# Memory attention with a SwiGLU block: values of batch 1 loaded ahead of the weights, summed transposed and scaled in U, and gates begun on the gate weights alone

## Chip, core and metric

One core of a Trainium2 chip runs the whole program. The time is that of one execution on the device in microseconds, as a median of several runs. A stage is timed inside a profiled execution, on that execution's own clock, which starts at its first instruction.

## The reference, cut to what matters

```python
# q, k, v: (8 batches, 8 heads, 576 tokens, 64)    phi: (8, 8, 576, 32 memories)
a = exp(phi);  a = a / sum(a over tokens)           # the maximum is taken off first; it cancels
k_m = einsum('bhsm,bhsd->bhmd', a, k);  v_m = einsum('bhsm,bhsd->bhmd', a, v)
attn = softmax(q @ k_m.T / 8 over the 32 memories);  x = heads of (attn @ v_m) side by side
g = x @ w_gate;  val = x @ w_val;  out = (silu(g) * val) @ w_out
```

The kernel never forms x. It multiplies each head's v_m by that head's 64 rows of the weights once per batch, which gives U, a matrix of (head, memory) by feature, and then g = attn @ U. U has to be built for the gate weights and for the value weights, in three chunks of 512 features.

## The kernel before

Batches 0 and 1 form the start: they are computed slot by slot, alternating, while the weights and all inputs still come in. A slot is one block of 128 features by 288 tokens: two matmuls for the gate, a Silu on ScalarE, two matmuls for the values, a product on VectorE. The value part of a slot runs one slot late. The parts that matter (cut):

```python
def v_items(b):                     # values: sum by (head, memory), divide, transpose
    def sums():
        p = ps.tile([128, NG * D], FP32, tag="b", name="p_kv")
        kv_sum(b, p, (1,))                                   # 48 matmuls
        v_norm(b, p.rearrange("p (g d) -> p g d", g=NG))     # VectorE, times 1/sum
    return [sums, lambda: kv_T(b, (1,))]                     # TensorE transpose, VectorE copy

def u_round(b, parts, evac):        # U of some weights: 8 matmuls, two PSUM banks a part
    ...
    for (t, p), e in zip(banks, evac):
        if e == "a":
            nc.scalar.copy(out=t, in_=p)
        else:
            nc.vector.tensor_copy(out=t, in_=p)

def gv_slot(b, s):                  # gate and Silu, then the value part of the slot before
    ...

# the schedule from the first U on
run([u_both_halves(0, 0, 0)])                      # gate and value weights, features 0 to 255
warm(6)                                            # dummies
run(g0[:3] + v1[:1] + g0[3:4] + v1[1:])            # batch 1's values amid batch 0's slots
run([u_both_halves(1, 0, 0)] + g1[:3])
...
for c in range(1, NCH):                            # features 512 to 1023, 1024 to 1535
    s = 8 * c
    run([u_item(0, c)] + g1[s - 2:s] + g0[s:s + 4])
    run([u_item(1, c)] + g0[s + 4:s + 8] + g1[s:s + 6])
```

PSUM gives six banks to all of this. A full U round (512 features, gate and value) takes four of them and gives them back when ScalarE and VectorE, two banks each, have copied them out. `warm(n)` is n dummy matmuls that keep TensorE running.

The softmax here doesn't subtract the row's maximum and nothing guards it: scores larger than these inputs give would overflow.

Of the kernel before, what the change touches and what calls it, by code (L numbers as in the profile page):

```python
# [14 lines left out]
def kernel(  # L15
# [48 lines left out]
    phis, kvs, qs, qTs = {}, {}, {}, {}  # L64
    Q_SLOT = (0, 1, 0, 0, 1, 0, 1, 0)

    def load_phi(b, eng):
        t = inp.tile([P, H, J * M], FP32, tag="phi", name="t_phi")
        eng.dma_start(out=t, in_=phi[b].rearrange("h (p j) m -> p h (j m)", p=P))
        phis[b] = t  # L70
# [80 lines left out]
    box = {}  # L151
# [110 lines left out]
    def k_items(b):  # L262


        def sums():
            box["k"] = ps.tile([128, NG * D + NG], FP32, tag="b", name="p_kv")
            kv_sum(b, box["k"], (0,))

        def norm():
            kv_denominators(b, box["k"], NG * D)  # L270
            kv_reciprocal(b, box["k"], NG * D)
            k_norm(b, box["k"][:, 0:NG * D].rearrange("p (g a d) -> p g a d", g=NG, a=1))

        return [sums, norm, lambda: kv_T(b, (0,))]

    def v_items(b):


        def sums():
            p = ps.tile([128, NG * D], FP32, tag="b", name="p_kv")  # L280
            kv_sum(b, p, (1,))
            v_norm(b, p.rearrange("p (g d) -> p g d", g=NG))

        return [sums, lambda: kv_T(b, (1,))]
# [65 lines left out]

    def u_round(b, parts, evac):

        banks = []
        for which, c, halves in parts:
            f0, f1 = HC * halves[0], HC * (halves[-1] + 1)
            p = [ps.tile([128, CH], FP32, tag="b", name=f"p_u{g}") for g in range(NG)]
            for i in range(NP):
                for g in range(NG):
                    nc.tensor.matmul(  # L359
                        p[g][32 * i:32 * i + 32, f0:f1],  # L360
                        lhsT=kTs[b][64 * g:64 * g + 64, 2, 32 * i:32 * i + 32],
                        rhs=W[which, c][64 * g:64 * g + 64, halves[0]:halves[-1] + 1, i],
                        start=True,
                        stop=True,
                        tile_position=(64 * g, 32 * i),
                    )
            for g in range(NG):
                if (b, which, c, g) not in Us:
                    Us[b, which, c, g] = upool.tile(
                        [128, CH], BF16, tag=f"U{which}{c}{g}", name="t_U"  # L370
                    )
                banks.append((Us[b, which, c, g][:, f0:f1], p[g][:, f0:f1]))
        for (t, p), e in zip(banks, evac):
            if e == "a":
                nc.scalar.copy(out=t, in_=p)  # L375
            else:
                nc.vector.tensor_copy(out=t, in_=p)  # L377
# [5 lines left out]
    def flush_mul():  # L383
        while pend:
            pend.pop(0)()

    def gv_half(b, s, which):
# [4 lines left out]
        for g in range(NG):  # L392
            nc.tensor.matmul(  # L393
                p[:, 0:HALF],
                lhsT=Us[b, which, c, g][:, 128 * o:128 * (o + 1)],
# [6 lines left out]
    def gv_slot(b, s):  # L402
# [5 lines left out]
        sg = work.tile([128, HALF], BF16, tag="sg", name="t_sg")  # L408
        nc.scalar.activation(out=sg, in_=gate, func=AF.Silu)  # L409
        flush_mul()  # L410
# [8 lines left out]

    def u_buffers(b):  # L420

        n = 0
        for which in range(2):
            for c in range(NCH):
                for g in range(NG):
                    Us[b, which, c, g] = hpool.tile([128, CH], BF16, tag=f"h{n}", name="t_U")
                    n += 1
# [88 lines left out]
    def u_item(b, c, evac="avav"):  # L516

        both = ((0, c, (0, 1)), (1, c, (0, 1)))
        return lambda: u_round(b, both, evac)

    def u_both_halves(b, c, half, evac="avav"):

        both = ((0, c, (half,)), (1, c, (half,)))
        return lambda: u_round(b, both, evac)

    def u_half(b, which, c, half, evac):
        return lambda: u_round(b, ((which, c, (half,)),), evac)


    def u_three(b):  # L530

        u_round(b, ((0, 0, (0, 1)), (1, 0, (0, 1)), (0, 1, (0, 1))), "avavav")

    def u_values(b):

        u_round(b, ((1, 1, (0, 1)),), "vv")
# [27 lines left out]
    load_phi(1, nc.scalar)  # L564
    load_k(0)
# [11 lines left out]
    for which in range(2):  # L577
        load_w(which, 0, 0)
    load_v(1)
    for which in range(2):  # L580
        load_w(which, 0, 1)
    for c in range(1, NCH):
# [15 lines left out]
    exp_tables()  # L598
    warm(140)
    phi_exp(0)  # L600
    phi_exp(1)
    k0, k1, v0, v1 = k_items(0), k_items(1), v_items(0), v_items(1)
    q0, q1 = q_items(0, "vava"), q_items(1, "vvvv")
    run(k0[:2])
    warm(8)
    run(k0[2:])
    warm(14)
    run(q0[:2])
    warm(5)
    scores(0, 0)  # L610
    run(q0[2:])
    warm(5)
    scores(0, 1)
    warm(3)
    z_inv(0, 0)
    run(k1[:2])
    run(q1[:1])
    z_inv(0, 1)
    run(k1[2:] + q1[1:2])
# [5 lines left out]
    z_inv(1, 0)  # L625
    warm(2)
    scores(1, 1)
    warm(17)
    z_inv(1, 1)
    norm(1, 0)  # L630
    nc.scalar.preload_act_table_set("silu_and_others")  # L631
    run(v0[:1])
    warm(8)
    run(v0[1:])
    norm(1, 1)


    g0, g1 = gv_slots(0), gv_slots(1)
    warm(6)
    run([u_both_halves(0, 0, 0)])  # L640
    warm(6)
    run(g0[:3] + v1[:1] + g0[3:4] + v1[1:])
# [109 lines left out]
```

## Time and profile before

| | before |
|---|---|
| median of the three runs known before the prediction (a fourth, in the first set, makes it 249.71) | 249.81 us (249.41 to 250.35) |
| first gate, profiled run | 27.38 us |
| first matmul of the output projection, which ends the stage of batches 0 and 1 | 57.28 us |
| span | 248.2 us |

### The profile page before, as it was taken

The numbers are of one execution on the slowest core, as the hardware profiler recorded it, in microseconds if no ns is written. First come the engines' busy times: TensorE is split into PE (matmuls) and PEld (weight loads), VectorE is DVE, ScalarE is ACT, GpSimd is POOL, SyncE is SP. The second block draws the span as 40 slices with busy tenths as digits, with TensorE's granted clock in tenths as the row PEclk, the third lists the DMA queues.
The fourth block names the chain that finished last, engine by engine and source line by source line (L and its number), as shares of the span: only waits on it lengthen the run. The fifth ranks groups of instructions, "written<-read, shape, count | busy, mean of one in ns | idle before, by whom it ended". The sixth has DMA issues, their size and how long they took to land.

```text
span 248.2 us, 6645 instructions
## 1 busy us (share of the span) xinstructions
PE 237.2 (96%) x2595; PEld 152.2 (61%) x2622; DVE 158.3 (64%) x339; ACT 166.0 (67%) x360; POOL 54.5 (22%) x85
## 2 busy tenths in 40 slices
PE   7999899999999999999999999999999999999993
PEld 7976566775544766467645666476546655467543
DVE  0027699994437788488856778478846876587420
ACT  2449688886077667966896577966896577676201
POOL 8434355000060002260505240080007000000000
PEclk9999999999999999999999999999999999999999
DMA  7999999999699973999699689589525311310143
GB/s 184 205 203 201 198 198 201 233 210 184 136 158 247 239 172 62 177 251 219 88 221 250 96 122 237 154 155 157 92 55 130 56 42 45 85 42 3 42 128 86
DMA packets 49168, 37.00 MB, mean 149 GB/s; under 512 B 15984, under 2 KB 43888, under 8 KB 49136
## 3 DMA queue, kind: packets, MB, share of 16 engines
q0 software_dynamic: 27632, 22.42, 57.1%
q1 hardware_dynamic: 20496, 13.37, 23.5%
q10 hardware_dynamic: 1008, 0.79, 1.2%
q8 instruction: 20, 0.33, 0.6%
q14 instruction: 12, 0.10, 0.1%
HBM read 42.47 MB, written 9.44 MB: 209 GB/s over the span
## 4 chain that ended last, share of the span: by engine, by line
PE 92%; ACT 3%; issue 2%; DVE 1%; DMA 1%
PE p_oo L449 35%; PE p_g L393 20%; PE p_v L393 19%; PE p_u L359 5%; PE p_oo L560 5%; PE p_kv L177 2%; PE p_g L316 1%; PE p_g L336 1%; DMA out_dram<-t_o 1%; PE p_v L336 1%; PE p_kv L197 1%; ACT L631 1%; ACT t_qT L303 0%; PE p_q L292 0%; PE p_T L241 0%
## 5 line engine op out<-in xcount | busy, mean ns | idle before, releaser
L449 PE MATMUL p_oo<-WO,t_h 128*128 128x512 bf16 x393 | 101.6, 379 | 3.0 <-issue 2.9
L409 ACT ACTIVATE t_sg<-p_g 128x288 bf16<-128x288 f32 x192 | 77.6, 413 | 32.3 <-PE p_g L393 24.6
L416 DVE TENSOR_TENSOR t_h<-t_sg,p_v 128x288 bf16<-128x288 bf16 x192 | 84.9, 452 | 20.5 <-PE p_v L393 16.0
L393 PEld LDWEIGHTS <-t_U 128*128 128x128 bf16 x768 | 74.0, 98 | 30.8 <-issue 1.4
L393 PE MATMUL p_g<-t_A,t_U 128*128 128x288 bf16 x384 | 78.0, 286 | 1.1 <-ACT t_U L375 0.7
L393 PE MATMUL p_v<-t_A,t_U 128*128 128x288 bf16 x384 | 77.2, 286 | 0.0
L449 PEld LDWEIGHTS <-t_h 128*128 128x128 bf16 x420 | 39.6, 98 | 41.0 <-issue 6.0
L377 DVE CAST t_U<-p_u 128x512 bf16<-128x512 f32 (+1 forms) x58 | 34.8, 646 | 7.3 <-PE p_u L359 7.3
L461 DVE COPY t_o<-p_oo 128x512 f32<-128x512 f32 x27 | 18.6, 690 | 31.4 <-PE p_oo L449 31.3
L375 ACT CAST t_U<-p_u 128x512 bf16<-128x512 f32 (+1 forms) x46 | 22.7, 554 | 10.8 <-PE p_u L359 10.6
L93 POOL DMA_DIRECT2D t_q<-in_q_dram x6 | 4.7, 780 | 63.0 <-DMA t_qT<-t_q 62.2
L560 PE MATMUL p_oo<-bones 128*128 128x128 bf16 x218 | 16.6, 240 | 1.5 <-DVE bones L572 1.5
L459 ACT COPY t_o<-p_oo 128x512 f32<-128x512 f32 x8 | 4.7, 588 | 19.7 <-PE p_oo L449 19.5
L359 PE MATMUL p_u<-W,t_kT 64*32 64x512 bf16 (+1 forms) x416 | 15.8, 365 | 0.7 <-DVE t_kT L243 0.7
L560 PEld LDWEIGHTS <-bones 128*128 128x128 bf16 x218 | 14.9, 109 | 2.3 <-DVE bones L572 1.5
L146 ACT ACTIVATE t_ephi<-t_phi 96x768 bf16<-96x768 f32 x16 | 12.5, 844 | 4.2 <-DMA t_phi<-in_phi_dram 4.2
L160 POOL COPY t_mark<-t_A 1x1 bf16<-1x1 bf16 x4 | 0.7, 180 | 52.5 <-DVE t_A L345 52.5
L207 DVE RECIPROCAL t_rS<-p_kv 128x2 f32<-128x2 f32 x8 | 1.4, 171 | 16.5 <-PE p_kv L197 13.6
L345 DVE TENSOR_TENSOR t_A<-t_E,t_lz 128x576 bf16<-128x576 bf16 x16 | 11.5, 750 | 0.4 <-ACT t_lz L340 0.4
L340 ACT ACTIVATE t_lz<-t_lz 128x576 f32<-128x576 f32 x16 | 10.9, 683 | 0.5
L164 POOL TENSOR_TENSOR t_es<-t_es,t_ephi 96x256 f32<-96x256 f32 x16 | 10.7, 667 | 1.3
L359 PEld LDWEIGHTS <-t_kT 64*32 64x32 bf16 x416 | 4.8, 89 | 9.5 <-issue 7.0
(52 smaller groups left out, 156.1 us busy)
## 6 DMA issues: line engine op xcount, KB each, us to landing
t_kv<-in_k_dram POOLq DMA_DIRECT2D x8, 576.0 KB, 10.1
t_kv<-in_v_dram POOLq DMA_DIRECT2D x8, 576.0 KB, 14.5
out_dram<-t_o SPq DMA_DIRECT2D x23, 192.0 KB, 3.0
t_phi<-in_phi_dram POOLq DMA_DIRECT2D x6, 576.0 KB, 15.5
t_q<-in_q_dram POOLq DMA_DIRECT2D x6, 576.0 KB, 7.9
out_dram<-t_o SPq DMA_DIRECT2D x24, 128.0 KB, 2.4
W<-in_moe_w_gate_dram POOLq DMA_DIRECT2D x6, 256.0 KB, 13.1
W<-in_moe_w_val_dram POOLq DMA_DIRECT2D x6, 256.0 KB, 12.7
```

The source lines that it names most:

```text
L146: nc.scalar.activation(out=t[:, :, g].rearrange("p j i m -> p i j m"), in_=src[:, g], func=AF.Exp)
L340: nc.scalar.activation(out=lz, in_=lz, func=AF.Exp, scale=-1.0)
L345: nc.vector.tensor_tensor(out=a, in0=es.pop((b, g)), in1=lzs.pop((b, g)), op=ALU.mult)
L359: nc.tensor.matmul(p[g][32 * i:32 * i + 32, f0:f1], lhsT=kTs[b][64 * g:64 * g + 64, 2, 32 * i:32 * i + 32], rhs=W[which, c][64 * g:64 * g ...
L375: nc.scalar.copy(out=t, in_=p)
L377: nc.vector.tensor_copy(out=t, in_=p)
L393: nc.tensor.matmul(p[:, 0:HALF], lhsT=Us[b, which, c, g][:, 128 * o:128 * (o + 1)], rhs=atts[b, g][:, r], start=(g == 0), stop=(g == NG - 1),)
L409: nc.scalar.activation(out=sg, in_=gate, func=AF.Silu)
L416: nc.vector.tensor_tensor(out=dst, in0=sg, in1=val, op=ALU.mult)
L449: nc.tensor.matmul(mine["p"], lhsT=hts[c, jf][:, 128 * u:128 * (u + 1)], rhs=WO[jf], start=(jf == 0), stop=(jf == NJF - 1),)
L461: nc.vector.tensor_copy(out=t_o, in_=mine["p"])
L560: nc.tensor.matmul(p[:, 0:128], lhsT=bones, rhs=bones, start=True, stop=True)
```

## The change

The intent is to get rid of the stop that batch 1's values make amid the first gates. Its v is loaded before the weights, so its sum can run before the first gate. The sum is built transposed, so that neither a division nor a TensorE transpose follows it; the division by the sum of a moves into U's copies, whose partitions are (head, memory). The first gates need only the gate weights' U, so they begin before the value weights have landed. Dummies fill TensorE up to there. The core of the diff, with cuts:

```diff
-        def sums():
-            p = ps.tile([128, NG * D], FP32, tag="b", name="p_kv")
-            kv_sum(b, p, (1,))
-            v_norm(b, p.rearrange("p (g d) -> p g d", g=NG))
-        return [sums, lambda: kv_T(b, (1,))]
+    def v_direct(b):
+        p = ps.tile([128, NP, M], FP32, tag="b", name="p_vT")
+        for i in range(NP):
+            for j in range(J):
+                for g in range(NG):
+                    nc.tensor.matmul(p[64 * g:64 * g + 64, i],
+                        lhsT=kvs[b][:, 1, 2 * i + g, j * D:(j + 1) * D],
+                        rhs=ephis[b][:, j, g, i], ...)
+        nc.vector.tensor_copy(out=kTs[b][:, 2], in_=p.rearrange("p i m -> p (i m)"))
+        scaled.add(b)
...
             if e == "a":
-                nc.scalar.copy(out=t, in_=p)
+                if r is None:
+                    nc.scalar.copy(out=t, in_=p)
+                else:
+                    nc.scalar.activation(out=t, in_=p, func=AF.Copy, scale=r)
+            elif r is None:
+                nc.vector.tensor_copy(out=t, in_=p)
             else:
-                nc.vector.tensor_copy(out=t, in_=p)
+                nc.vector.tensor_scalar(out=t, in0=p, scalar1=r, scalar2=None, op0=ALU.mult)
...
     load_v(0)
-    for which in range(2):
-        load_w(which, 0, 0)
     load_v(1)
-    for which in range(2):
-        load_w(which, 0, 1)
-    for c in range(1, NCH):
+    for c in range(NCH):
         for half in range(2):
             for which in range(2):
                 load_w(which, c, half)
...
-    run([u_both_halves(0, 0, 0)])
-    warm(6)
-    run(g0[:3] + v1[:1] + g0[3:4] + v1[1:])
-    run([u_both_halves(1, 0, 0)] + g1[:3])
-    run([u_both_halves(0, 0, 1)] + g1[3:4] + g0[4:7])
-    run([u_both_halves(1, 0, 1)] + g0[7:8] + g1[4:6])
+    v_direct(0)
+    ...
+    warm(24)
+    v_direct(1)
+    warm(4)
+    run([u_half(0, (0,), 0, 0, "av"), u_half(1, (0,), 0, 0, "av")])
+    warm(6)
+    for s in range(4):
+        gv_gate(0, s)
+    run([u_half(0, (1,), 0, 0, "va"), u_half(1, (1,), 0, 0, "va")])
+    for s in range(2):
+        gv_gate(1, s)
+    flush_mul(3)
+    run([u_half(0, (0, 1), 0, 1, "va")])
+    flush_mul(2)
+    run(g1[2:4])
+    run([u_half(1, (0, 1), 0, 1, "av")] + g0[4:8] + g1[4:5])
     for c in range(1, NCH):
         s = 8 * c
-        run([u_item(0, c)] + g1[s - 2:s] + g0[s:s + 4])
-        run([u_item(1, c)] + g0[s + 4:s + 8] + g1[s:s + 6])
+        run([u_item(0, c)] + g1[s - 3:s] + g0[s:s + 5])
+        run([u_item(1, c)] + g0[s + 5:s + 8] + g1[s:s + 5])
```

U is also laid out with gate and value in one tile, for all batches. Further up, the denominators go ahead of k's sum, q's copies of batch 0 all go to VectorE, and 130 dummies open the program in place of 140.

More of the change, by code (lines that the diff above doesn't have):

```diff
@@ L64, with load_phi @@
     phis, kvs, qs, qTs = {}, {}, {}, {}
+    box = {}
     Q_SLOT = (0, 1, 0, 0, 1, 0, 1, 0)
-    def load_phi(b, eng):
+    def load_phi(b, *engs):
         t = inp.tile([P, H, J * M], FP32, tag="phi", name="t_phi")
-        eng.dma_start(out=t, in_=phi[b].rearrange("h (p j) m -> p h (j m)", p=P))
+        n = H // len(engs)
+        for i, eng in enumerate(engs):
+            eng.dma_start(
+                out=t[:, n * i:n * (i + 1)],
+                in_=phi[b, n * i:n * (i + 1)].rearrange("h (p j) m -> p h (j m)", p=P),
+            )
         phis[b] = t
@@ L149, in phi_exp @@
         ephis[b] = t
-    box = {}
     esums = {}
@@ L262, in k_items, with denominators @@
     def k_items(b):
-        def sums():
-            box["k"] = ps.tile([128, NG * D + NG], FP32, tag="b", name="p_kv")
-            kv_sum(b, box["k"], (0,))
-        def norm():
-            kv_denominators(b, box["k"], NG * D)
-            kv_reciprocal(b, box["k"], NG * D)
-            k_norm(b, box["k"][:, 0:NG * D].rearrange("p (g a d) -> p g a d", g=NG, a=1))
-        return [sums, norm, lambda: kv_T(b, (0,))]
-    def v_items(b):
+        def denominators():
+            p = ps.tile([128, NG], FP32, tag="b", name="p_S")
+            kv_denominators(b, p, 0)
+            kv_reciprocal(b, p, 0)
         def sums():
             p = ps.tile([128, NG * D], FP32, tag="b", name="p_kv")
-            kv_sum(b, p, (1,))
-            v_norm(b, p.rearrange("p (g d) -> p g d", g=NG))
-        return [sums, lambda: kv_T(b, (1,))]
+            kv_sum(b, p, (0,))
+            k_norm(b, p.rearrange("p (g a d) -> p g a d", g=NG, a=1))
+        return [denominators, sums, lambda: kv_T(b, (0,))]
+    def v_direct(b):
[3 more added lines that the diff above has]
+                for g in range(NG):
+                    nc.tensor.matmul(
+                        p[64 * g:64 * g + 64, i],
+                        lhsT=kvs[b][:, 1, 2 * i + g, j * D:(j + 1) * D],
+                        rhs=ephis[b][:, j, g, i],
+                        start=(j == 0),
+                        stop=(j == J - 1),
+                        tile_position=(0, 64 * g),
+                    )
+        nc.vector.tensor_copy(out=kTs[b][:, 2], in_=p.rearrange("p i m -> p (i m)"))
+        scaled.add(b)
     def q_T(b, g, n, eng="v"):
@@ L349 @@
     Us = {}
+    scaled = set()
     def u_round(b, parts, evac):
@@ L354, in u_round @@
         for which, c, halves in parts:
-            f0, f1 = HC * halves[0], HC * (halves[-1] + 1)
-            p = [ps.tile([128, CH], FP32, tag="b", name=f"p_u{g}") for g in range(NG)]
-            for i in range(NP):
-                for g in range(NG):
-                    nc.tensor.matmul(
-                        p[g][32 * i:32 * i + 32, f0:f1],
-                        lhsT=kTs[b][64 * g:64 * g + 64, 2, 32 * i:32 * i + 32],
-                        rhs=W[which, c][64 * g:64 * g + 64, halves[0]:halves[-1] + 1, i],
-                        start=True,
-                        stop=True,
-                        tile_position=(64 * g, 32 * i),
-                    )
@@ L367, in u_round @@
-            for g in range(NG):
-                if (b, which, c, g) not in Us:
-                    Us[b, which, c, g] = upool.tile(
-                        [128, CH], BF16, tag=f"U{which}{c}{g}", name="t_U"
-                    )
-                banks.append((Us[b, which, c, g][:, f0:f1], p[g][:, f0:f1]))
-        for (t, p), e in zip(banks, evac):
-            if e == "a":
-                nc.scalar.copy(out=t, in_=p)
+            w0, w1, h0, h1 = which[0], which[-1] + 1, halves[0], halves[-1] + 1
@@ new lines, in u_round @@
+            n = (h1 - h0) * HC
+            p = [
+                ps.tile([128, 2, HC], FP32, tag="b", name=f"p_u{g}").rearrange("p a f -> p (a f)")
+                for g in range(NG)
+            ]
+            for w in which:
+                o = (w - w0) * n
+                for i in range(NP):
+                    for g in range(NG):
+                        nc.tensor.matmul(
+                            p[g][32 * i:32 * i + 32, o:o + n],
+                            lhsT=kTs[b][64 * g:64 * g + 64, 2, 32 * i:32 * i + 32],
+                            rhs=W[w, c][64 * g:64 * g + 64, h0:h1, i],
+                            start=True,
+                            stop=True,
+                            tile_position=(64 * g, 32 * i),
+                        )
@@ new lines, in u_round @@
+            for g in range(NG):
+                if (b, c, g) not in Us:
+                    Us[b, c, g] = upool.tile([128, 2, 2, HC], BF16, tag=f"U{c}{g}", name="t_U")
+                if len(which) == 1:
+                    dst = Us[b, c, g][:, h0:h1, w0]
+                else:
+                    dst = Us[b, c, g][:, h0]
+                src = p[g][:, 0:(w1 - w0) * n].rearrange("p (a f) -> p a f", f=HC)
+                banks.append((dst, src, rSs[b][:, g, 0] if b in scaled else None))
+        for (t, p, r), e in zip(banks, evac):
+            if e == "a":
+                if r is None:
+                    nc.scalar.copy(out=t, in_=p)
+                else:
+                    nc.scalar.activation(out=t, in_=p, func=AF.Copy, scale=r)
+            elif r is None:
+                nc.vector.tensor_copy(out=t, in_=p)
@@ L376, in u_round, with flush_mul @@
             else:
-                nc.vector.tensor_copy(out=t, in_=p)
+                nc.vector.tensor_scalar(out=t, in0=p, scalar1=r, scalar2=None, op0=ALU.mult)
     hts = {}
     pend = []
-    def flush_mul():
-        while pend:
+    def flush_mul(n=None):
+        for _ in range(len(pend) if n is None else n):
             pend.pop(0)()
@@ L394, in gv_half @@
                 p[:, 0:HALF],
-                lhsT=Us[b, which, c, g][:, 128 * o:128 * (o + 1)],
+                lhsT=Us[b, c, g][:, o // 2, which, 128 * (o % 2):128 * (o % 2 + 1)],
                 rhs=atts[b, g][:, r],
@@ L400, in gv_half, with gv_gate @@
         return p[:, 0:HALF]
-    def gv_slot(b, s):
+    def gv_gate(b, s):
         jf, r = s // 2, s % 2
@@ L407, in gv_slot @@
         gate = gv_half(b, s, 0)
-        sg = work.tile([128, HALF], BF16, tag="sg", name="t_sg")
+        sg = work.tile([128, HALF], BF16, tag="sg", bufs=8, name="t_sg")
         nc.scalar.activation(out=sg, in_=gate, func=AF.Silu)
-        flush_mul()
         col = (b % 2) * S + r * HALF
@@ L418, in gv_slot @@
         pend.append(mul)
+    def gv_slot(b, s):
+        n = len(pend)
+        gv_gate(b, s)
+        flush_mul(n)
     def u_buffers(b):
-        n = 0
-        for which in range(2):
-            for c in range(NCH):
-                for g in range(NG):
-                    Us[b, which, c, g] = hpool.tile([128, CH], BF16, tag=f"h{n}", name="t_U")
-                    n += 1
+        for c in range(NCH):
+            for g in range(NG):
+                Us[b, c, g] = hpool.tile([128, 2, 2, HC], BF16, tag=f"h{2 * c + g}", name="t_U")
     def token_segments(t0, count):
@@ L516, in u_item @@
     def u_item(b, c, evac="avav"):
-        both = ((0, c, (0, 1)), (1, c, (0, 1)))
-        return lambda: u_round(b, both, evac)
-    def u_both_halves(b, c, half, evac="avav"):
-        both = ((0, c, (half,)), (1, c, (half,)))
-        return lambda: u_round(b, both, evac)
+        return lambda: u_round(b, (((0,), c, (0, 1)), ((1,), c, (0, 1))), evac)
     def u_half(b, which, c, half, evac):
@@ L530, in u_three @@
     def u_three(b):
-        u_round(b, ((0, 0, (0, 1)), (1, 0, (0, 1)), (0, 1, (0, 1))), "avavav")
+        u_round(b, (((0,), 0, (0, 1)), ((1,), 0, (0, 1)), ((0,), 1, (0, 1))), "avavav")
     def u_values(b):
-        u_round(b, ((1, 1, (0, 1)),), "vv")
+        u_round(b, (((1,), 1, (0, 1)),), "vv")
     def run(items):
@@ L564 @@
     load_phi(1, nc.scalar)
+    exp_tables()
+    phi_exp(0)
+    phi_exp(1)
     load_k(0)
@@ L576 @@
     load_v(0)
-    for which in range(2):
-        load_w(which, 0, 0)
     load_v(1)
-    for which in range(2):
-        load_w(which, 0, 1)
-    for c in range(1, NCH):
+    for c in range(NCH):
         for half in range(2):
@@ L595 @@
     u_buffers(1)
-    exp_tables()
-    warm(140)
-    phi_exp(0)
-    phi_exp(1)
-    k0, k1, v0, v1 = k_items(0), k_items(1), v_items(0), v_items(1)
-    q0, q1 = q_items(0, "vava"), q_items(1, "vvvv")
+    warm(130)
+    k0, k1 = k_items(0), k_items(1)
+    q0, q1 = q_items(0, "vvvv"), q_items(1, "vvvv")
     run(k0[:2])
     warm(8)
-    run(k0[2:])
-    warm(14)
+    run(k0[2:] + k1[:1])
+    warm(10)
     run(q0[:2])
-    warm(5)
+    warm(3)
     scores(0, 0)
     run(q0[2:])
-    warm(5)
+    warm(2)
+    z_inv(0, 0)
     scores(0, 1)
     warm(3)
-    z_inv(0, 0)
-    run(k1[:2])
-    run(q1[:1])
+    run(k1[1:2])
     z_inv(0, 1)
-    run(k1[2:] + q1[1:2])
+    warm(2)
+    run(k1[2:] + q1[:2])
     warm(4)
@@ L624 @@
     norm(0, 1)
-    z_inv(1, 0)
     warm(2)
     scores(1, 1)
-    warm(17)
+    z_inv(1, 0)
     z_inv(1, 1)
+    v_direct(0)
+    nc.scalar.preload_act_table_set("silu_and_others")
     norm(1, 0)
-    nc.scalar.preload_act_table_set("silu_and_others")
-    run(v0[:1])
-    warm(8)
-    run(v0[1:])
     norm(1, 1)
+    warm(24)
+    v_direct(1)
+    warm(4)
     g0, g1 = gv_slots(0), gv_slots(1)
+    run([u_half(0, (0,), 0, 0, "av"), u_half(1, (0,), 0, 0, "av")])
     warm(6)
-    run([u_both_halves(0, 0, 0)])
-    warm(6)
-    run(g0[:3] + v1[:1] + g0[3:4] + v1[1:])
-    run([u_both_halves(1, 0, 0)] + g1[:3])
-    run([u_both_halves(0, 0, 1)] + g1[3:4] + g0[4:7])
-    run([u_both_halves(1, 0, 1)] + g0[7:8] + g1[4:6])
+    for s in range(4):
[8 more added lines that the diff above has]
+    run([u_half(1, (0, 1), 0, 1, "av")] + g0[4:8] + g1[4:5])
     for c in range(1, NCH):
         s = 8 * c
-        run([u_item(0, c)] + g1[s - 2:s] + g0[s:s + 4])
-        run([u_item(1, c)] + g0[s + 4:s + 8] + g1[s:s + 6])
-    run(g1[-2:])
+        run([u_item(0, c)] + g1[s - 3:s] + g0[s:s + 5])
+        run([u_item(1, c)] + g0[s + 5:s + 8] + g1[s:s + 5])
+    run(g1[-3:])
     flush_mul()
```

## The prediction

> **What bounds the kernel now.** I read the page first: the busy row of TensorE by slice, and the chain that ended last.
>
> ```profile
> PE   7999899999999999999999999999999999999993
> PEclk9999999999999999999999999999999999999999
> DMA  7999999999699973999699689589525311310143
> PE 92%; ACT 3%; issue 2%; DVE 1%; DMA 1%
> L560 PE MATMUL p_oo<-bones 128*128 128x128 bf16 x218 | 16.6, 240 | 1.5 <-DVE bones L572 1.5
> ```
>
> TensorE carries 92% of the chain at an undiminished clock, and from the first gate on it is nearly gapless. But 218 of its matmuls are dummies (16.6 us, all before 27.4 us): the start is no TensorE work. A change that touches only the start can shift the whole rest, and by no more than the first gates move. The changed lines for batches 2 to 7 only lay the same U out differently. So I went to the start: the chain in order of time around the first gate.
>
> ```profile
> 24.22 0.72 ACT t_lz L339 x2
> 24.96 0.68 ACT t_lz L340
> 25.66 1.28 ACT L631
> 26.96 0.38 ACT t_U L375
> 27.38 0.67 PE p_g L393 x4
> ...
> 28.78 0.49 PE p_kv L177 x48
> ...
> 29.97 0.46 DVE t_h L416
> 30.62 0.38 PE p_u L359 x9
> 30.99 0.37 ACT t_U L375
> 31.41 0.42 PE p_g L393 x2
> ```
>
> The first gate waits for U's copy on ScalarE, which waits for the table load (1.28 us), which waits for the last softmax normalisation. Then the values of batch 1 are summed at 28.78, amid the gates: sum, normalise, transpose, copy, U, copy. TensorE stops for most of 29.9 to 31.4. Next, GpSimd's timeline, where each load waits for the landing of the one eight places before it, so its waits tell when loads land:
>
> ```profile
> 22.64 0.74 POOL L118 DMA_DIRECT2D W<-in_moe_w_gate_dram  x1 [1.80 <-DMA t_kv<-in_v_dram]
> 23.98 0.74 POOL L118 DMA_DIRECT2D W<-in_moe_w_val_dram  x1 [0.59 <-DMA W<-in_moe_w_gate_dram]
> 25.32 0.74 POOL L118 DMA_DIRECT2D W<-in_moe_w_gate_dram  x1 [0.61 <-DMA W<-in_moe_w_val_dram]
> 28.34 0.74 POOL L118 DMA_DIRECT2D W<-in_moe_w_val_dram  x1 [2.27 <-DMA t_kv<-in_v_dram]
> 29.63 0.74 POOL L118 DMA_DIRECT2D W<-in_moe_w_gate_dram  x1 [0.56 <-DMA W<-in_moe_w_gate_dram]
> 30.97 0.74 POOL L118 DMA_DIRECT2D W<-in_moe_w_val_dram  x1 [0.60 <-DMA W<-in_moe_w_val_dram]
> ```
>
> By these waits v of batch 0 landed at about 22.5, the first halves of gate and value weights at 23.8 and 25.2, v of batch 1 at 28.2, the second halves at 29.5 and 30.8 (0.15 us taken off each for the semaphore; the DMA view's issue plus duration gives the same, e.g. 11.67 + 16.4 = 28.1). So the batch 1 sum at 28.71 followed its data by half a microsecond: the start is paced by transfers as much as by arithmetic. A 256 KB half takes 1.3 us, a 576 KB v 3.0.
>
> **What the Trainium skill says.** "DMA: Bandwidth & Descriptors", section "Anatomy of one DMA — SWDGE (gpsimd) path", says that DMA engines do not wait on semaphores and just consume their queues; the landings above, in order of issue, agree, so swapping two loads swaps their times and gains no bandwidth. "TensorE: Matmul & The Clock Gate", section "Weight-path perf modes — Fast Weight Load (FWL) and DoubleRow", gives fast weight load only to weights of 128 columns, and its section "LDWEIGHTS (loading the stationary operand)" makes load time grow with columns: the new sum loads 64 columns each time where the old one loads 32. It states columns/1.2 ns. The trace shows overlap across column tiles: 48 load-and-multiply pairs of the old sum started within 0.48 us (28.71 to 29.20), 10 ns each. "VectorE: DVE Perf Modes", section "Why PSUM operands drop a tier", holds fp32 from PSUM to one element a cycle, for a copy as for a multiply by a scalar; I therefore price the scaled copies like the old: 0.65 us for 512 columns on VectorE, 0.55 on ScalarE.
>
> **The change part by part.** For batches 0 and 1 the sum of v by head, its normalisation, a transpose and a copy become one transposed sum and a copy; the division moves into U's copies, where it costs nothing by the paragraph above. Gone per batch: one VectorE multiply (0.29 us), one TensorE transpose, and two hand-overs between engines.
>
> Loads. v of batch 1 goes ahead of the first weights: v1 at 22.5 + 3.0 = 25.5, gate half at 26.8, value half at 28.1; from there all is as before (29.5, 30.8; the last piece of the second 512 columns at 23.98 + 12.1 = 36.1). So the gate weights come 3.0 us later, v1 2.7 sooner.
>
> Before the first gate. 130 dummies for 140: 10 x 0.074 = 0.74 us earlier. Denominators ahead of k's sum take the reciprocal off the chain (0.2 us); q's copies all go to VectorE, which unloads ScalarE. Redoing the chain with the lags of this trace (copy to scores 0.05, scores to Exp 0.34, Exp to sum 0.05, sum to Ln 0.32, pairs on ScalarE 0.31 apart) I get the scores of batch 0 at 15.2 and 16.8 (before 15.85 and 17.5) and those of batch 1 at 20.2 and 21.8 (before 21.0 and 22.6). Now both Exp of batch 1 stand ahead of both Ln. ScalarE then runs 22.2 Exp, 22.8 Ln, 23.5 Exp, 24.1 Ln, 24.9 to 25.5 Exp, table load to 26.85: of 0.7 us gained, 0.1 is left.
>
> TensorE after that: v_direct(0) starts at 23.1. Its 48 matmuls I put at 0.8 us, between 0.48 (the old rate) and 1.3 (64 columns/1.2 ns, two tiles at once, an estimate from the skill's formula). Then 24 dummies (1.8), v_direct(1) at 25.7 to 26.5 (v1 is there at 25.5), its copy to 26.75, four dummies. Gate U of batch 0 starts near 26.8, where its weights have just landed; 0.36 to the copy (as at 30.62 to 30.98), 0.4 for it: first gate at about 27.65, before 27.38. That is 0.3 us later.
>
> After the first gate. Before: 27.38 to the end of the stage at 57.5 is 30.1 us: 48 slots of four matmuls at 0.49 = 23.5, three half U rounds at 0.53 and four full ones at 0.72 = 4.5, the v1 sum 0.6, the stop around its transpose 1.0, small waits 0.5. After: the same 23.5 and 4.5 (both batches' value U, 16 matmuls together, is one half round), no sum, no stop, small waits 0.5: 28.5, so 27.65 + 28.5 = 56.15. One new wait: the second 512 columns would begin at 27.65 + 12.5 slots x 0.49 + 3 x 0.53 + 0.2 = 35.6, but their last weights land at 36.1; the gate half of that round runs meanwhile, so I charge 0.3. End of stage 56.45, against 57.5: 1.0 us gained. Copies of whole 512 columns for two of 256 save a few tenths on VectorE and ScalarE, which bound nothing. I take 0.1 back for bank waits of gates ahead of values (six PSUM banks, four held by gates, two by U): 0.9.
>
> After that stage everything is TensorE in order. Batch 2's q lands at 62.8 in either kernel and its transposed form at 67.8, while its scores stand at 70.16; moved 0.9 earlier they still clear it by 1.5. So the gain should reach the end: 249.8 - 0.9 = 248.9.
>
> **The rivals.**
>
> *The start is bound by transfers or dummies, and the gain is given back.* Weights three microseconds later, 24 + 4 + 6 dummies and a v_direct of 1.3 instead of 0.8 (twice, in series) would put the first gate at 28.4 to 28.9; the 0.3 wait vanishes, but 0.5 to 1.0 is lost: 249.3 to 249.8. For it: loads are in place half a microsecond before use. Against: the dummies fill time that waits anyway.
>
> *Gates ahead of values jam.* Four Silu at about 0.37 stand before the value copies on ScalarE, and values wait for these copies; TensorE then stops near 29.8 for up to 0.8. For it: ScalarE is the first engine busy there. Against: the value copies start on VectorE for one half of the heads, and two gates of batch 1 fill the wait. Time: 249.4.
>
> *The whole stop goes and no wait replaces it.* Gate at 27.4, no wait for the second columns: 1.4 gained, 248.4.
>
> *Later batches slow* by U's strided halves: 512-column copies would cost more than 0.65 and 0.55. In the later stages VectorE and ScalarE are about two thirds busy, so I expect nothing.
>
> **Range and chances.** Middle 248.9. The spread of the rivals is 248.4 to 249.8, and three executions before span 249.41 to 250.35, which argues for a low end of 248.1 and a high end of 249.8. The 2% border is 5 us, more than all that the start can lose or gain: within 2% 0.96, faster 0.02, slower 0.02 for something unseen in the layout or clock.
>
> **What would show it.** Gate weights landing near 26.8 and v1 near 25.5; v_direct about 0.8 us for 48; table load ending near 26.85; first gate near 27.65; no TensorE gap of over half a microsecond from 29 to 32; stage end near 56.5; batch 2's stage as before, one microsecond earlier. I am wrong if the first gate comes after 28.3, if TensorE stops at the values near 30 or at the second columns near 36, or if something after 57 eats the shift.

## More of the kernel before

The lines that carry the argument are shown in the prediction. Two more are needed later: the groups of U's copies in the window of that stage, by shape. The columns are line, engine, operation, output and input, count, then total busy time and the mean ns of one.

```profile
L377 DVE CAST t_U<-p_u 128x512 bf16<-128x512 f32 x8 | 5.1, 681 | 0.0
L375 ACT CAST t_U<-p_u 128x512 bf16<-128x512 f32 x8 | 4.3, 589 | 0.8 <-PE p_u L359 0.8
```

A plain copy of 512 columns takes 681 ns on VectorE (DVE) and 589 on ScalarE (ACT).

## The result, and the profile after

The first four runs gave 249.55 us (249.37 to 249.94) against 249.71, a ratio of 0.9992 with an interval of 0.9968 to 1.0016. Ratios here are the mean time of one kernel's fast runs over that of the other's in the same rounds, so not quite the ratio of the medians. A later set of five rounds on the same kernel gave 0.9977 (0.9965 to 0.9989), a gain of about 0.6 us. So the change helps, within 2%, by less than the predicted 0.9; the first set alone does not show it.

The profile page of the changed kernel, the same rows as the prediction shows of the one before:

```profile
PEclk9999999999999999999999999999999999999998
PE 87%; DMA 8%; POOL 2%; issue 2%; ACT 0%; POOLq 0%
L588 PE MATMUL p_oo<-bones 128*128 128x128 bf16 x198 | 15.7, 244 | 1.5 <-DVE bones L603 1.5
```

TensorE's share of the chain fell from 92 to 87%, and a transfer stands in it with 8%. That is the load of batch 1's v, which the chain in order of time shows:

```profile
6.98 18.77 DMA t_kv<-in_v_dram
25.79 0.94 PE p_vT L290 x48
...
27.06 0.36 PE p_u L383 x16
27.42 0.44 PE p_oo L588 x6
27.89 1.15 PE p_g L425 x8
29.04 0.36 PE p_u L383 x16
...
35.82 0.34 PE p_u L383 x8
36.23 0.41 PE p_u L383 x8
```

Read from the top: v lands at 25.75 us (6.98 plus 18.77), the direct sum follows at once, U at 27.06, and eight gate matmuls run unbroken from 27.89. The stop of the kernel before, from 29.9 to 31.4, is gone. At 36.23 the second half of the U round for the next 512 features waits a little for the last weights, as predicted.

The stage ends at 56.88 us (before: 57.28), and from there to the end of the span it is 190.7 us in the changed kernel and 190.9 in the kernel before. So the result was made in the stage, as predicted, but it is 0.4 there and not 1.0. (The prediction's 57.5 and 56.45 are the end of the last gate or value matmul, which is 57.44 before and 57.04 after: 0.4 by that marker too.) The copies show a difference that the prediction had priced at nothing:

```profile
L409 DVE TENSOR_SCALAR t_U<-p_u,t_rS 128x512 bf16<-128x512 f32 x10 | 7.1, 744 | 0.0
L405 ACT ACTIVATE t_U<-p_u,t_rS 128x512 bf16<-128x512 f32 x10 | 6.4, 685 | 1.4 <-PE p_u L383 1.4
```

A scaled copy takes 63 ns more than a plain one on VectorE and 96 ns more on ScalarE. And TensorE's own timeline shows full U rounds, with eight slots between one and the next, further apart than they should be (columns: start, duration, engine, line, operation):

```profile
40.62 0.62 PE L383 MATMUL p_u<-W,t_kT 64*32 64x512 bf16 x16
45.50 0.63 PE L383 MATMUL p_u<-W,t_kT 64*32 64x512 bf16 x16
```

That is 4.88 us for eight slots and a round. In the kernel before, these rounds are unevenly spaced, four slots and six, so the fair figure is two of them:

```profile
37.48 0.62 PE L359 MATMUL p_u<-W,t_kT 64*32 64x512 bf16 x16
...
46.81 0.63 PE L359 MATMUL p_u<-W,t_kT 64*32 64x512 bf16 x16
```

The sum of 2 and 4 slots, then 4 and 6, is 16 slots and two rounds in 9.33 us, or 4.67 each. So a round costs 0.21 us more after the change. Two things differ around a round: the kind of copy, and which slots stand behind it.

### The profile page after: what moved, and what is told of

It is laid out like the page before. It is cut to its first block, busy times and chain, and to the rows that moved or that the text cites. A ratio compares the mean times of both kernels' runs of the same rounds, so it can differ in the third digit from the quotient of the medians.

```text
span 247.6 us, 6587 instructions
## 1 busy us (share of the span) xinstructions
PE 237.5 (96%) x2573; PEld 152.3 (61%) x2600; DVE 158.9 (64%) x337; ACT 165.2 (67%) x356; POOL 54.5 (22%) x85
## 4 chain that ended last, share of the span: by engine, by line
PE 87%; DMA 8%; POOL 2%; issue 2%; ACT 0%; POOLq 0%
PE p_oo L483 36%; PE p_g L425 20%; PE p_v L425 19%; DMA t_kv<-in_v_dram 8%; PE p_u L383 6%; PE p_kv L183 2%; PE p_oo L514 1%; POOL t_q L93 1%; POOL t_kv L81 1%; PE p_g L351 1%; PE p_v L351 1%; PE p_g L331 1%; PE p_vT L290 0%; PE p_kv L203 0%; PE p_oo L588 0%
## 5 line engine op out<-in xcount | busy, mean ns | idle before, releaser
L495 DVE COPY t_o<-p_oo 128x512 f32<-128x512 f32 x27 | 18.6, 690 | 31.4 <-PE p_oo L483 31.3
L407 DVE CAST t_U<-p_u 128x512 bf16<-128x512 f32 x42 | 26.7, 684 | 6.8 <-PE p_u L383 6.8
L403 ACT CAST t_U<-p_u 128x512 bf16<-128x512 f32 x30 | 15.8, 592 | 8.9 <-PE p_u L383 8.9
L588 PE MATMUL p_oo<-bones 128*128 128x128 bf16 x198 | 15.7, 244 | 1.5 <-DVE bones L603 1.5
L588 PEld LDWEIGHTS <-bones 128*128 128x128 bf16 x198 | 13.9, 111 | 2.1 <-DVE bones L603 1.5
L341 ACT ACTIVATE t_E<-p_g 128x288 bf16<-128x288 f32 x16 | 6.6, 412 | 8.5 <-PE p_v L331 7.9
```

The lines of the kernel that those rows point to most:

```text
L495: nc.vector.tensor_copy(out=t_o, in_=mine["p"])
L588: nc.tensor.matmul(p[:, 0:128], lhsT=bones, rhs=bones, start=True, stop=True)
```

## The experiments

Theory 1: the scaled copies cost the gain, because Silu and products queue behind them and TensorE waits for banks. Theory 2: the new order of slots around the rounds makes the waits. Theory 3, formed after the first set: a later transfer takes gain back. Theory 1 was shown in the end for the copies, but the queue of Silu turned out not to be what TensorE waits for; see "Plain on ScalarE". The stage end in the last column is the first matmul of the output projection in the profiled run.

| run | median, us | ratio to before (95%) | first gate | full rounds apart, per 8 slots | stage end |
|---|---|---|---|---|---|
| before (first set) | 249.71 | | 27.38 | 4.67 | 57.28 |
| changed | 249.55 | 0.9992 (0.9968 to 1.0016) | 27.89 | 4.88 | 56.88 |
| changed, again | 249.42 | 0.9977 (0.9965 to 0.9989) | 27.75 | 4.88 | 56.78 |
| unscaled copies (wrong result) | 249.42 | 0.9978 (0.9961 to 0.9994) | 27.63 | 4.67 | 56.19 |
| before, scaled by one | 250.61 | 1.0030 (1.0015 to 1.0045) | 26.55 | 4.87 | 57.77 |
| scale in the softmax | 248.94 | 0.9970 (0.9953 to 0.9986) | 28.19 | 4.67 | 56.71 |
| slots as before | 249.45 | 0.9984 (0.9970 to 0.9998) | 27.80 | 4.88 | 56.78 |
| plain on ScalarE (wrong result) | 249.01 | 0.9971 (0.9951 to 0.9991) | 27.76 | 4.70 | 56.55 |
| softmax and slots | 248.81 | 0.9964 (0.9949 to 0.9979) | 27.94 | 4.67 | 56.05 |
| with early loads | 250.96 | 1.0062 (1.0036 to 1.0088) | 27.73 | 4.67 | 55.84 |
| changed, with early loads | 251.04 | 1.0054 (1.0039 to 1.0070) | 27.82 | 4.88 | 57.16 |
| v behind the first weights | 253.07 | 1.0142 (1.0121 to 1.0163) | 30.46 | 4.88 | 60.38 |
| v ahead of q | 248.52 | 0.9944 (0.9932 to 0.9956) | 27.82 | 4.67 | 55.91 |
| no late dummies | 250.97 | 1.0031 (1.0017 to 1.0044) | 28.03 | 4.88 | 58.44 |

### Unscaled copies

```diff
         nc.vector.tensor_copy(out=kTs[b][:, 2], in_=p.rearrange("p i m -> p (i m)"))
-        scaled.add(b)
```

> The changed kernel with U's copies of batches 0 and 1 left unscaled; the result is wrong on purpose (the values of these two batches are not divided by their sums). Theory 1, the scaled copies cost the gain: copies of 512 columns fall back to 0.59 us on ScalarE and 0.68 on VectorE, the three waits of about 0.2 us after the U rounds at 40.7, 45.6 and 50.5 shrink to about 0.05, and the stage of the first two batches ends about 0.4 to 0.6 us sooner than in the changed kernel (first 26-matmul block of the output projection at 56.8 in place of 57.3); time about 249.1. Theory 2, the new order of slots around the U rounds (3 and 5 in place of 2 and 4) makes the waits: they stay, and the time stays at 249.5.

The copies fell back to 587 and 683 ns, the rounds stood 4.67 us apart, and the stage ended 0.7 us sooner, of which 0.26 is an earlier first gate in that execution; against it, the wait for the weights at 36.2 was longer there (0.33 us). The waits went without a change of order, as theory 1 says. The median, however, was 249.42 and not the expected 249.1: in the time of the whole program this run shows no gain over the changed kernel. In the profiled run the gain of the stage was lost later, at the sum for batch 3:

```profile
86.21 0.85 PE L183 MATMUL p_kv<-t_kv,t_ephi 96*32 96x128 bf16 x48 [0.75 <-DMA t_kv<-in_v_dram]
```

TensorE arrived early and waited 0.75 us for v of batch 3. This is where theory 3 comes from. But the profiled execution was the slowest of the six (249.76), so it does not tell what the median lost.

### Before, scaled by one

```diff
+                if b < 2:
+                    nc.scalar.activation(out=t, in_=p, func=AF.Copy, scale=onesf)
...
+            elif b < 2:
+                nc.vector.tensor_scalar(out=t, in0=p, scalar1=onesf, scalar2=None, op0=ALU.mult)
```

> The kernel before with only the kind of U's copies changed: those of batches 0 and 1 are multiplied by a column of ones, result unchanged. Theory 1 (the scaled copies are dearer, and TensorE feels it): 0.69 and 0.74 us a copy of 512 columns, waits after the four full U rounds grow from about 0.1 to about 0.3 us, the half rounds lose some too; stage end 0.6 to 1.0 us later (58.3 to 58.7 in place of 57.7), time about 250.5. Theory 2 (order of slots): waits unchanged, time 249.7.

The kernel before, with nothing changed but the kind of copy, lost 0.3%:

```profile
37.15 0.63 PE L360 MATMUL p_u<-W,t_kT 64*32 64x512 bf16 x16
...
46.89 0.63 PE L360 MATMUL p_u<-W,t_kT 64*32 64x512 bf16 x16
```

Two rounds take 9.74 in place of 9.33 us, 0.205 each. Its first gate was even 0.8 us sooner than in the profile of before (TensorE's first 140 dummies took 9.28 us there against 10.42), and still the stage ended 0.5 later. The expected 58.3 to 58.7 was counted from the block of 26 matmuls, 0.43 later than the marker of the table, so it means 57.9 to 58.3, which the early start missed by 0.1; the mechanism and the time (250.5 expected, 250.61 measured) agree with theory 1, and theory 2 has no part in this run.

### Scale in the softmax

```diff
-        scaled.add(b)
...
-        nc.vector.tensor_tensor(out=a, in0=es.pop((b, g)), in1=lzs.pop((b, g)), op=ALU.mult)
+        if b < 2:
+            nc.vector.scalar_tensor_tensor(
+                out=a, in0=lzs.pop((b, g)), scalar=rSs[b][:, g, 0], in1=es.pop((b, g)),
+                op0=ALU.mult, op1=ALU.mult,
+            )
```

> The changed kernel with the division moved on into the softmax normalisation of batches 0 and 1 (a VectorE operation with a scalar and two tensors), U's copies plain, result right. Theory 1: as with unscaled copies, stage end near 56.8 and time near 249.1, provided that the operation takes about the 0.75 us of the one it replaces. Theory 2: no change from 249.5.

The attention weights have the same partitions as U, so the division can go there, four operations that took 811 ns each in place of 751. The result is right, and the rounds are back at 4.67:

```profile
41.08 0.62 PE L388 MATMUL p_u<-W,t_kT 64*32 64x512 bf16 x16
45.75 0.62 PE L388 MATMUL p_u<-W,t_kT 64*32 64x512 bf16 x16
```

The ratio is 0.9970, although in the profiled run v landed late and the first gate came at 28.19.

### Slots as before

```diff
-    run([u_half(1, (0, 1), 0, 1, "av")] + g0[4:8] + g1[4:5])
+    run([u_half(1, (0, 1), 0, 1, "av")] + g0[4:8] + g1[4:6])
...
-        run([u_item(0, c)] + g1[s - 3:s] + g0[s:s + 5])
-        run([u_item(1, c)] + g0[s + 5:s + 8] + g1[s:s + 5])
+        run([u_item(0, c)] + g1[s - 2:s] + g0[s:s + 4])
+        run([u_item(1, c)] + g0[s + 4:s + 8] + g1[s:s + 6])
...
```

> The changed kernel with the order of slots around the U rounds as before (2 and 4, then 4 and 6), scaled copies kept. It also puts one more slot ahead of the second 512 columns, so the wait there of 0.4 us for the last weights should go under either theory. Theory 1: the waits after the rounds stay, stage end 0.3 to 0.4 us sooner than in the changed kernel (57.0), time 249.2. Theory 2: the waits after the rounds go too, stage end 56.4, time 248.6.

Rounds at 36.15 and 45.90, 9.75 us for two: with scaled copies the order makes no difference, and theory 2 falls. The wait for the last weights is gone (one round of 0.63 us where the changed kernel had 0.89), but the stage ended at 56.78, only 0.1 sooner: the first full round, which in the changed kernel cost no bank waits after its pause for weights, now has them too. The expected 57.0 was counted from the block of 26 matmuls, 0.43 later than the marker of the table, so it means 56.6 and was missed by 0.2; the time, 249.45, missed the expected 249.2 likewise.

### Plain on ScalarE

```diff
-                if r is None:
-                    nc.scalar.copy(out=t, in_=p)
-                else:
-                    nc.scalar.activation(out=t, in_=p, func=AF.Copy, scale=r)
+                nc.scalar.copy(out=t, in_=p)
```

> The changed kernel with only ScalarE's copies of U plain (0.59 us) and VectorE's still scaled (0.74); the result is wrong on purpose. If the Silu queued behind ScalarE's two copies hold TensorE back (1.27 us a pair scaled, 1.07 plain: 0.20, as large as the 0.21 that a round lost), the distance from round to round returns from 4.88 to 4.67 us, stage end near 56.2 to 56.4, time 249.0. If VectorE's pair (1.40 in place of 1.28) holds it, the distance stays at 4.8 or more and the time at 249.4.

The pair of copies on ScalarE and the third gate after the round, in the changed kernel and in this one:

```profile
41.10 1.27 ACT L405 ACTIVATE t_U<-p_u,t_rS 128x512 bf16<-128x512 f32 x2 [0.20 <-PE p_u L383]
...
42.42 0.40 PE L425 MATMUL p_g<-t_A,t_U 128*128 128x288 bf16 x2
```

```profile
41.30 1.07 ACT L402 CAST t_U<-p_u 128x512 bf16<-128x512 f32 x2 [0.20 <-PE p_u L383]
...
42.43 0.41 PE L422 MATMUL p_g<-t_A,t_U 128*128 128x288 bf16 x2
```

The rounds moved to 4.70 us apart with VectorE's copies still scaled. So 0.18 of the 0.21 us is ScalarE's pair (0.20 longer). The traces also tell what TensorE waits for, though they name no wait there. In the 29 full rounds of eight kernels that did not wait for weights, the second gate starts 0.05 us after ScalarE's first copy ends, and the third 0.05 us after its second: here 41.10 plus 1.27 is 42.37, and the gate starts at 42.42. So these gates take the banks that the two copies free. The Silu queued behind the pair, which theory 1 and this expectation name, are not it: the first runs from 42.26 to 42.67 in the changed kernel, and the third gate starts before it is done. The stage end of 56.55 misses the 56.2 to 56.4 because this execution waited 0.42 us for value weights near 31.4.

### Softmax and slots

Both edits together.

> The changed kernel with both of the last edits: the division in the softmax normalisation (plain copies of U) and the order of slots as before (no wait for the second 512 columns). Theory 1 by itself: 0.21 us saved at each of four full rounds, some 0.1 at each half round, 0.3 at the wait: stage end near 55.9 (changed kernel 56.88), time near 248.5. Theory 3, a later transfer caps the gain: v of batch 3 lands at 85.5 to 86.2 in every run so far, since its load is issued only near 70, behind a load of q that waits for the transposition of batch 2's q; the sum that reads it stood at 86.5 in the kernel before and 86.1 in the changed one. By theory 3 TensorE waits there for 0.8 to 1.2 us in this run and the time stays near 248.9 to 249.1, as with the division moved alone.

The stage end was 56.05, 1.2 us before that of the kernel before, and the time 248.81. In the profiled execution the sum of batch 3 started at 85.25 without a wait, so theory 3's wait of 0.8 to 1.2 did not show in it; the median of 248.81 lies between what theory 1 alone (248.5) and the cap (248.9 to 249.1) expected. This run did not decide theory 3. Its premise was also misread: v of batch 3 did not land at 85.5 or later in every run so far, but at 84.7 with the scale in the softmax and at 84.9 with the slots as before, so that only the unscaled run had met it. For theory 1 the run is a clean pair with "slots as before", from which it differs only in where the division sits: from the first gate to the end of the stage it takes 28.11 us, and the other 28.98.

### With early loads, on that kernel and on the changed one

```diff
     load_q(2)
+    load_k(3)
+    load_v(3)
     load_q(3)
...
         if b == 2:
-            load_k(3)
-            load_v(3)
```

> The same with k and v of batch 3 loaded ahead of q of batch 3, so that they don't stand behind the wait for the transposition. Theory 3: no wait at the sum of batch 3, the whole gain of the stage reaches the end, time 248.2 to 248.5 (1.2 to 1.5 us below the kernel before). Against it: the two loads fall on the transposition of batch 2's q and delay it beyond 69, which would make a new wait at batch 2's scores; then 249 again.

> The changed kernel with only the early loads of k and v of batch 3. Theory 3 says that in the changed kernel that sum (86.1) comes some 0.5 us after its v, so that nothing is taken back there in the executions seen: time 249.5 as the changed kernel, at most 0.1 to 0.2 less. If the time falls to 249.0 or below, the cap had already taken part of the changed kernel's gain and the scaled copies explain less of the shortfall.

Both failed, and both at the place that the expectation of the first named as the danger. The loads fell on the transposition of batch 2's q by the DMA queue of SyncE, which issues for 5.67 us in place of 3.07, and TensorE waited for its result:

```profile
70.87 0.28 PE L330 MATMUL p_g<-t_qT,t_kT 64*32 64x288 bf16 x1 [1.96 <-DMA t_qT<-t_q]
```

On the changed kernel the same wait was 0.56, and the sum of batch 3 came at 87.55 in place of 86.08; what took the rest of that was not followed. So the second run says nothing about the cap it was meant for; it shows that a gain in the stage is worth what the transfers after it allow.

### v ahead of q

```diff
     load_q(2)
-    load_q(3)
...
         if b == 2:
+            mark = att.tile([1, 1], BF16, tag="markq", bufs=1, name="t_markq")
+            nc.gpsimd.tensor_copy(out=mark, in_=qTs[2, 0][0:1, 0, 0:1])
             load_k(3)
             load_v(3)
+            load_q(3)
```

> The kernel with the division in the softmax and the old order of slots, and now k and v of batch 3 still loaded after the transposition of batch 2's q (GpSimd reads one element of its result first), but ahead of q of batch 3. v lands some 2.5 to 3 us sooner (near 82.5), no transposition is disturbed. If v of batch 3 was a cap on part of the executions, the slow ones of the last set go: median 248.5 to 248.7, narrower. If it was not, 248.8 as without.

GpSimd reads one element of the transposed q, and only then issues k, v and q of batch 3 in this order. v was issued at 69.03 and landed 12.6 us later, at 81.6 (before: 69.98 and 15.6 us, 85.6); nothing disturbed the transposition. The time fell to 248.52, ratio 0.9944: the fastest of all versions, 1.4 us below the kernel before. Against softmax and slots (0.9964), which ran in another set, the intervals overlap a little, so what this last step adds is not shown. In the profiled runs it added nothing: from the end of the stage to the end of the span it is 190.8 us in both. Nor did the slow executions go, as the expectation had it: two of five took 248.9.

### v behind the first weights, and no late dummies

```diff
     load_v(0)
-    load_v(1)
     for c in range(NCH):
         for half in range(2):
             for which in range(2):
                 load_w(which, c, half)
+            if c == 0 and half == 0:
+                load_v(1)
```

> The changed kernel with the order of loads undone: v of batch 1 behind the first halves of the weights, as before, the program of TensorE unchanged. Its v then lands near 28.2 in place of 25.6, and the direct sum of batch 1 stands ahead of the first U, so the first gate comes at about 30.3 in place of 27.9; the wait of 0.4 for the second 512 columns is absorbed. Stage end 58.8 to 59.0, time 251.4 to 251.6. If it is much less, the order of the loads is not what lets the gates begin.

The sum of batch 1 started at 28.20 after a wait of 3.22 us and the first gate at 30.46, both as expected. But the time was 1.5 us longer than expected. The eight first gate matmuls took 2.13 us in place of 1.15, because TensorE's clock had been halved. Stretches of that run show when (from and to, length, then busy time of TensorE, its weight loads, VectorE, ScalarE and GpSimd, then the granted clock, DMA share and rate):

```profile
25.00:28.20 3.20, 0.00 (x2) 0.01 (x2) 0.68 (x1) 1.19 (x1) 0.74 (x1) 1.00 1.37 199
28.20:29.60 1.40, 1.40 (x68) 1.25 (x68) 0.29 (x1) 0.00 (x0) 0.74 (x1) 1.00 1.45 196
29.60:33.00 3.40, 3.40 (x46) 1.86 (x38) 0.88 (x3) 2.44 (x6) 2.02 (x3) 0.50 1.45 198
```

The wait itself passed at full clock; the clock fell 1.4 us after work had begun again, and stayed low for 3.4 us. The other run takes the dummies away and leaves the loads:

```diff
-    warm(24)
     v_direct(1)
-    warm(4)
...
     run([u_half(0, (0,), 0, 0, "av"), u_half(1, (0,), 0, 0, "av")])
-    warm(6)
```

> The changed kernel without the 34 dummies between the direct sum of batch 0 and the first gate. If they are only filler, TensorE waits longer for v of batch 1 and the first gate stays at 27.9, time 249.5. If they hold the clock, TensorE idles 1.9 us before v, the granted clock falls, and the first gates run at half speed as in the run with v behind the weights (8 gate matmuls in 2.1 us in place of 1.15): 1 to 1.5 us later, time 250.5 to 251.0.

Here v landed as in the changed kernel, and TensorE had nothing to do for 1.88 us before. First its timeline, then its stretches (columns as above):

```profile
25.63 1.47 PE L290 MATMUL p_vT<-t_ephi,t_kv 96*64 96x32 bf16 x48 [1.88 <-DMA t_kv<-in_v_dram]
...
28.03 2.10 PE L425 MATMUL p_g<-t_A,t_U 128*128 128x288 bf16 x8
```

```profile
24.00:26.00 2.00, 0.37 (x14) 0.37 (x16) 1.50 (x3) 1.95 (x4) 0.13 (x1) 0.72 1.44 196
26.00:30.00 4.00, 3.82 (x66) 2.28 (x62) 1.23 (x3) 2.54 (x6) 2.35 (x4) 0.50 1.45 196
```

The granted clock fell to 0.50 at 24.9, 1.1 us into the pause, and stayed there to 31.7, through the first gates, which began at 28.03, nearly as early as with dummies, but ran at half speed. The stage ended 1.6 us later. The 34 dummies compute nothing, and they are worth more than the whole change gains (1.5 us against 0.6). The first gate came only 0.14 us later than with them, so nearly all of the loss lies in the stretch at half clock.

### Changed, again

> The changed kernel itself once more, for a tighter time: the sum of what the other runs showed (0.21 us more at each full U round, a first gate 0.5 later, no stop for batch 1's values) gives 0.3 to 0.5 us below the kernel before; ratio 0.998 to 0.999.

0.9977, at the near end of the expected range. In the profiled run the stage ended at 56.78.

## Why the prediction was right or wrong

Right, with the numbers of the changed kernel's profiled run:

- The transfers. v of batch 1 expected at 25.5: its sum started at 25.79. GpSimd's waits put the gate weights at 26.9 (26.8 expected) and the value weights at 28.2 (28.1 expected), as swapping the order of loads had it.
- The direct sum: 0.87 us to the next instruction (0.8 expected).
- ScalarE's table load ended at 26.68 (26.85 expected), and ceased to matter: U's copies began at 27.36.
- The first gate: 27.89 (27.65 expected), 0.24 of the gain lost. The sum waited for its v to 25.79, and the rest follows it; nearly 0.1 of the difference is the scaled copy itself (0.48 us where 0.4 was put).
- No stop at batch 1's values, and no jam of gates ahead of values: TensorE was busy without a gap of half a microsecond from 28 on.
- The wait for the second 512 features: near 36.2, about 0.3.
- The stage carried to the end: 190.7 and 190.9 us remain. The late copies of the other batches, in the new layout, took 684 and 592 ns, against 683 and 592 before.

That the time fell inside the range is partly luck. 249.55, and 249.42 in the second set, lie 0.5 to 0.65 above the middle, where two rivals stood (start bound, 249.3 to 249.8; gates jam, 249.4); neither of them happened. The first gate was not after 28.3, and no jam came. What filled their place was a cost that the prediction had set to nothing.

Wrong, in size: the term "I therefore price the scaled copies like the old: 0.65 us for 512 columns on VectorE, 0.55 on ScalarE", together with the line that these engines "bound nothing". They took 0.744 and 0.685, which is 0.06 and 0.10 more than a plain copy in the same stage (the 0.65 and 0.55 were the page's means over copies of 512 and of 256 columns mixed, 646 and 554 ns; of 512 alone a plain one took 681 and 589), and each of three full rounds after 40 us lost 0.21, together 0.63; the half rounds about 0.1 more (28.97 to 30.90 from one to the next, against 28.71 to 30.55 with unscaled copies). Shown, for the stage, by five runs: plain copies bring the rounds back to 4.67 wherever the division goes, scaled copies bring them to 4.87 in the kernel before as well, the order of slots does nothing, and ScalarE's pair alone accounts for 0.18. The other terms of the stage came out some 0.4 better than predicted, which is why it ended only 0.6 later than expected (57.04 for 56.45), of which 0.24 is the first gate. The averaged loads of 64 and 67% hid the cost: in the stage itself (27.3 to 57.7) VectorE was busy 90% and ScalarE 83% of the time before the change, and behind a U round it is the banks of ScalarE's copies that TensorE mostly waits for, for some 0.3 us each time (4.88 less eight slots of 0.49, the round's 0.56 and 0.11 after it).

The price was to be had beforehand. The prediction took the VectorE page for both engines; the Trainium skill has ScalarE's case in "ScalarE: Activation LUTs", section "What ACT_TABLE_LOAD costs": each [128,1] pointer operand of an ACTIVATE adds about 93 ns. The trace agrees: 96 (685 against 589).

The statement that the gain reaches the end without loss held for the changed kernel by a margin of some 0.5 us: its sum of batch 3 stood at 86.08 and v at 85.5. The prediction had checked the transposed q of batch 2, with 1.5 us to spare, and not v of batch 3, which is issued behind it. The one profiled execution of the run with unscaled copies met that bound. How much it costs on average, over executions whose transfers vary by half a microsecond, stays open.

## What to carry to other kernels

A scale folded into a PSUM copy isn't free: price the operand, and ask not how loaded the engine is on average but who waits for the bank that the copy frees. Fold a per-partition factor into an operation that waits for nothing, here the softmax normalisation. In the stage that was worth 0.2 us a full round; over the whole program 0.9970 against 0.9977 does not separate the two. When the start of a kernel is paced by transfers, list the landing time of every later load before counting a gain through to the end, and keep TensorE turning while it waits: 34 dummies were worth 1.5 us here.

## What the Trainium skill lacked or had wrong

- "VectorE: DVE Perf Modes": no page was found that prices a per-partition scalar operand on VectorE. Here it added 63 ns to a copy of 512 columns (681 to 744), 62 to one of 256 (418 to 480), and 60 to a product of two tensors of 576 columns (751 to 811): a cost that does not grow with the elements. No run separates the operand from the change of operation that comes with it (a copy becomes a product).
- "TensorE: Matmul & The Clock Gate", section "What's actually happening": it gives the idle clock after at least one idle window of about 3.4 us. Here no pause was that long, and still the clock fell. In the run without late dummies it went to 0.50 at 24.9, and in the 3.4 us before that TensorE was busy for 2.1; with v behind the weights it went down at 29.6, after 3.4 us of which TensorE was busy for 1.4. The page does not say how much work keeps the clock up.
- The same page, section "LDWEIGHTS (loading the stationary operand)": columns/1.2 ns gives 53 ns for one load of 64 columns, and the prediction's estimate, with two column tiles loading at once, 1.3 us for 48. The record of one such load is 113 ns (96 for 32 columns), and the direct sum took 0.87 us, 18 ns for a load and its matmul. The formula fits neither figure, and this section does not say how loads overlap.
